# A fused linear attention and MoE kernel: the queries of batches 3 to 7 projected once, by token, and their exponentials turned by DMA transposes

## The chip, the core and the metric

The kernel runs on one core of one Trainium2 chip. The metric is the device time of one execution in microseconds (us), median of several runs. Engines are named as in the profile: PE is TensorE (PEld its weight loads), DVE is VectorE, ACT is ScalarE, POOL is GpSimd, and SP is SyncE, whose in-order queue issues nearly all DMAs.

## The reference

Attention with a feature map comes first, then a two-layer network over its output:

```
def phi(x):
    proj = np.einsum('bhsd,df->bhsf', x, w_phi)
    proj = proj - np.max(np.abs(proj), axis=-1, keepdims=True)
    return np.concatenate([np.exp(proj), np.exp(-proj)], axis=-1)
q_p, k_p = (phi(q), phi(k))
kv = np.einsum('bhsf,bhsd->bhfd', k_p, v)
z = np.sum(k_p, axis=2)
num = np.einsum('bhsf,bhfd->bhsd', q_p, kv)
den = np.einsum('bhsf,bhf->bhs', q_p, z)[..., None] + 1e-06
...
h = x @ w_in
g = h * (1.0 / (1.0 + np.exp(-1.702 * h)))
return (g @ w_out).astype(np.float32)
```

There are 8 batches, 8 heads, 576 tokens, head dimension 64 and 128 features, so phi gives 256. The second part takes 4608 tokens of 512 channels through 2048 hidden units. Here it is called the MoE, after the names of its weights.

## The kernel before

Each float32 operand is held as two f16 parts, high and low (`eh` and `el` for an exponential `e`), and a product is three f16 products: high by high, high by low, low by high.

**Attention** goes by batch and by pair of heads. `attn_load` fetches a pair's `kt`, `qt` and `vn` (512 of the 576 tokens; the last 64 tokens of all heads are done once per batch by `attn_tail`). `turned` splits `qt` or `kt` into two parts (`xs`) and turns them by one DMA transpose into `xT`, channels on partitions, eight tiles of 128 tokens. `keys` makes the sums `kz`. `queries` takes the eight tiles of queries in two halves of four. For each half, `project_q` projects **twice**. `by_token` gives the projection with tokens on partitions (eight passes of 128 columns with `xT` as weights), and VectorE takes the largest magnitude `m` of each token from it. Two further passes of 512 columns, with `ph` as weights, give the same projection turned: features on partitions, in a second PSUM bank `pT`. `features_q` takes the two exponentials of `pT` and their parts, and these serve as weights in `numden`, which multiplies them with `kz`. `token_scales` uses `m` to set each token's scale afterwards.

```
def project_q(xT, m, bank, also=()):
    pp3 = by_token(xT, bank, ())
    R.vector.tensor_reduce(m, pp3, AX.X, ALU.max, apply_absolute_value=True)
    pT = psa()
    mv = xT.rearrange("p t s -> p (t s)")
    R.tensor.matmul(pT, ph[:, 0], mv, start=True, stop=False, also=also)
    R.tensor.matmul(pT, ph[:, 1], mv, start=False, stop=True)
    return pT
```

**The MoE** goes over 384 tokens at a time (`moe_chunk`), 16 hidden blocks `j` for each: passes into a bank `hb`, then tanh (`th`) on ScalarE, `g` on VectorE, the parts `gh` and `gl`, and passes into three banks `ab`. One block `j` of one chunk is called a step here; there are 208 of them. Each step has one `g` and one `gl` instruction on VectorE, by which a place in the program can be found in any version. The attention of batches 3 to 7 is interleaved with the MoE of earlier batches.

**Order.** All instructions are first recorded (`Recorder`), then put in order by a list scheduler (`schedule`). It takes priorities from a table (`PLACES`), prices each instruction, gives out buffers, and chooses the engine where there is a choice: `two` means VectorE or GpSimd, `three` also ScalarE. Each engine then executes its instructions in that order. SP's queue too is in order: a DMA whose source isn't ready holds up all that stand behind it. `touch` finds which earlier instructions an instruction must follow.

The weights are loaded through three buffers `raw` (4 KB a partition) and two buffers `wy` (2 KB).

Of the kernel before, what the change touches and what calls it, by code (L numbers as in the profile page):

```python
# [10 lines left out]
F16 = mybir.dt.float16  # L11
# [5 lines left out]
AF = mybir.ActivationFunctionType  # L17
ALU = mybir.AluOpType
AX = mybir.AxisListType
PSUM = bass.MemoryType.PSUM  # L20

P = 128
# [3 lines left out]
LN2 = math.log(2.0)  # L26
# [4 lines left out]
class _Buf:  # L31


    def __init__(self, aps, ordered):
        self.aps, self.ordered = aps, ordered
        self.avail = [0.0] * len(aps)
        self.owner = [None] * len(aps)
        self.queue, self.head = [], 0

# [138 lines left out]
class Recorder:  # L178
# [63 lines left out]
    def claim(self, o, tl):  # L242
        if tl not in o.uses:
            if tl.first is None:
                tl.first = o
                o.allocs.append(tl)
            else:
                o.deps.setdefault(tl.first, False)
            o.uses.append(tl)
            tl.left += 1  # L250

    def touch(self, o, a, write):
        tl = a.tl
        self.claim(o, tl)
        p0, p1, rs = a.region()
        keep = []
        for ent in tl.log:
            (q0, q1, cs), w, d = ent
            hit = q0 < p1 and p0 < q1 and any(c0 < b1 and b0 < c1 for b0, b1 in rs for c0, c1 in cs)
            if hit and (w or write) and d is not o:  # L260
                o.deps[d] = True
            over = write and d is not o and p0 <= q0 and q1 <= p1
            if not (over and all(any(b0 <= c0 and c1 <= b1 for b0, b1 in rs) for c0, c1 in cs)):
                keep.append(ent)
        keep.append(((p0, p1, rs), write, o))
        tl.log = keep
# [207 lines left out]
def attn_moe_fast(ctx, tc, q, k, v, w_phi, w_in, w_out, out):  # L474
# [21 lines left out]
    U = 1.0 / PH  # L496
    EK, EQ, KZ = 3, 8, 13
# [4 lines left out]
    R = Recorder(nc)  # L502

    def buf(name, shape, dt, n, pool=cp, ordered=True):
        return _Buf(
            [pool.tile(shape, dt, tag=f"{name}{i}", name=f"{name}{i}") for i in range(n)],
            ordered,
        )

    def static(name, shape, dt):  # L510
# [12 lines left out]
        xT=([P, 8, P], F16), tl=([P, 3, NHP, D], F32), t=([P, 4, NF], F32),   # L523
        e=([P, 512], F32), eh=([P, 512], F16), el=([P, 512], F16),
# [7 lines left out]
        wy=([P, DM], F32), zt=([P, 2, NHP, 2, D], F16),  # L532
    )
    loose = ("sc", "eh", "el", "e", "n1", "cs", "rc", "mq")
    pools = {
        nm: buf(nm, sh, dt, NB[nm], ordered=nm not in loose) for nm, (sh, dt) in shapes.items()
    }

    def new(nm):
        return R.tile(pools[nm])  # L540
# [12 lines left out]
    def psa():  # L553
        return R.tile(at, whole=True)
# [98 lines left out]
    def weight_max(i):  # L653
        R.vector.tensor_reduce(
            wmx[:, i : i + 1], w16[:, i, 0], AX.X, ALU.max, apply_absolute_value=True
        )

    def w1(j, part, ct):
        return w16[:, 2 * j, part, ct * P : (ct + 1) * P]

# [29 lines left out]
    def turned(n, g=None):  # L690


        j = 8 if g is None else 4
        xs_, xT = new("xs")[:, 0:j], new("xT")[:, 0:j]
        h, l = xs_[:, :, 0], xs_[:, :, 1]
        if g is not None:
            n = halved(n, g)
            h, l = (x.rearrange("p (a j) d -> p a j d", a=2) for x in (h, l))
        R.three.copy(h, n)
        R.two.tensor_sub(l, n, h)  # L700
        R.sync.dma_start_transpose(xT, xs_.rearrange("p s i d -> p (s i d)"))
        return xT

    def by_token(xT, bank, also):
        pp = bank()
        for t in range(4):
            o = pp[:, t * NF : (t + 1) * NF]
            st = xT[:, t]
            R.tensor.matmul(o, st, ph[:, 0], start=True, stop=False, also=also)
            R.tensor.matmul(o, st, ph[:, 1], start=False, stop=True)  # L710
        return pp.rearrange("p (a f) -> p a f", a=4)
# [11 lines left out]
# [8 lines that stand above are left out]
# [33 lines left out]
    def features_q(pT, hi="eh", lo="el"):  # L764


        pr = []
        for sg in (U, -U):
            e, h, l = new("e"), new(hi), new(lo)
            R.scalar.activation(e, pT, AF.Exp, scale=sg, bias=-EQ * LN2)  # L770
            R.three.copy(h, e)
            R.two.tensor_sub(l, e, h)
            pr.append((h, l))
        return pr

    def token_scales(m, n):

        cs = new("cs")[:, :, 0:n]
        R.scalar.activation(cs[:, 0], m, AF.Exp, scale=-2.0 * U, bias=-EK * LN2)
        R.scalar.activation(cs[:, 1], m, AF.Exp, scale=-U, bias=EPD)  # L780
        return cs
# [121 lines left out]
    def numden(kz, st, mv, n, c, dst, more=()):  # L903


        nd = psa()[:, 0 : n * 2 * DV].rearrange("p (j s d) -> p j s d", j=n, s=2)
        mm = []
        for s in range(2):
            for i in range(len(st)):
                (eh, el), r = st[i][s], mv[i]  # L910
                o = nd[:, i, s] if len(st) == n else nd[:, :, s]
                a, z = (kz[:, x, r, s] for x in range(2))
                mm += [(eh, a, o), (eh, z, o), (el, a, o)]
        for w, z in more:
            mm.append((w, z, nd[:, :, 1, D + 1]))
        products(mm, (dst,))
        n1 = new("n1")[:, 0:n]
        R.evac.copy(n1, nd[:, :, 0])
        R.two.tensor_mul(n1, n1, c.unsqueeze(2).broadcast_to([P, n, DV]))
        R.vector.tensor_add(dst, nd[:, :, 1], n1)  # L920
# [57 lines left out]
    def queries(hp, qt_, kz, nt, x16, bank, g=None):  # L978


        n = 8 if g is None else 4
        w = n // 2
        nf = new("nf")[:, 0:n]
        xT = turned(qt_, g)
        m = new("mq")[:, 0:n]
        eq = [
            features_q(project_q(xT[:, h : h + 4], m[:, h : h + 4], bank, (nf,)))
            for h in range(0, n, 4)
        ]
        cs = token_scales(m, n)  # L990
        for s0, c in ((0, 3), (3, 3), (6, 2)) if g is None else ((0, 2), (2, 2)):
            sl = range(s0, s0 + c)
            numden(
                kz,
                [[[e[:, x % 4 * P : x % 4 * P + P] for e in eq[x // 4][s]] for s in range(2)]
                 for x in sl],
                [x // w for x in sl],
                c,
                cs[:, 0, s0 : s0 + c],
                nf[:, s0 : s0 + c],  # L1000
            )
        rc = new("rc")[:, 0:n]
        R.two.tensor_add(rc, nf[:, :, D], cs[:, 1])
        R.vector.reciprocal(rc, rc)
        xj = divided(nf, rc, w)
        if g is not None:
            turned_back(xj, hp, x16, g)
        else:
            xo = new("xo")
            R.three.copy(xo[:, 0], xj)  # L1010
            R.two.tensor_sub(xo[:, 1], xj, xo[:, 0])
            for t in range(2):
                R.sync.dma_start_transpose(
                    x16[:, t, hp, 0:MAIN].rearrange("p (j t) -> p j t", t=P),
                    xo[:, t].rearrange("p j c -> p (j c)"),
                )
        ratio(rc.rearrange("p (h j) -> p h j", h=2),
              nt[:, 2 * hp : 2 * hp + 2, D + 1].unsqueeze(2).broadcast_to([P, 2, w]),
              art[:, 0, 0:n].rearrange("p (h j) -> p h j", h=2))
# [170 lines left out]
    def v_att(i):  # L1190
        if i < 4:
            return VA[0][0] + VA[0][1] * i
        if i < 8:
            return VA[1][0] + (i - 4) * VA[1][1]
        return VA[2][0] + (i - 8) * VA[2][1]
# [7 lines left out]
    def attention(b):  # L1203
        u = v_att(4 * b)
        x16 = place(b)
        R.part(u - 0.01, u)
        tl = tail_load(b)
        nt = new("nt")
        R.part(u, u + 0.266)
        tail = attn_tail(b, tl, psa)  # L1210
        for hp in range(NHP):
            w = v_att(4 * b + hp)
            R.part(w, w + 0.517)
            kt, qt, vn = attn_load(b, hp)
            kf, kz = keys(b, hp, kt, vn, tail, nt, b == 1 and EXK1[hp], False, psa)
            queries(hp, qt, kz, nt, x16, psa)
            if hp == NHP - 1:
                queries_tail(nt, tail[3], x16)
# [54 lines left out]
    kept = new("x").rearrange("p t c s -> p (t c s)").bitcast(F32)  # L1273
    kept = kept[:, 0 : 4 * DM].rearrange("p (i n) -> p i n", i=4)
    attention(2)

    for part_ in range(NH):
        for c in (0, 256):
# [199 lines left out]
```

## Time and profile before

| | |
|---|---|
| time, median of 3 runs | 1052.39 us (1051.38 to 1053.2) |
| span of the profiled execution, first to last instruction | 1050.8 us |
| PE busy | 1010.8 us (96%) |
| PEld busy | 666.7 us (63%) |
| DVE busy | 734.5 us (70%) |
| ACT busy | 652.1 us (62%) |
| POOL busy | 283.4 us (27%) |
| DMA queue of SP and ACT issues, share of 16 engines | 30.8% |

The profiled execution has no timed value of its own beyond its span. The runs lie 0.6 to 2.4 us above it, the median 1.6 us. A busy share is an average over stretches with different limits, and the end of a matmul is modelled; how closely passes follow each other is read from their starts.

### The profile page before, as it was taken

The numbers are of one execution on the slowest core, as the hardware profiler recorded it, in microseconds if no ns is written. First come the engines' busy times: TensorE is split into PE (matmuls) and PEld (weight loads), VectorE is DVE, ScalarE is ACT, GpSimd is POOL, SyncE is SP. The second block draws the span as 40 slices with busy tenths as digits, with TensorE's granted clock in tenths as the row PEclk, the third lists the DMA queues.
The fourth block names the chain that finished last, engine by engine and source line by source line (L and its number), as shares of the span: only waits on it lengthen the run. The fifth ranks groups of instructions, "written<-read, shape, count | busy, mean of one in ns | idle before, by whom it ended". The sixth has DMA issues, their size and how long they took to land.

```text
span 1050.8 us, 24672 instructions
## 1 busy us (share of the span) xinstructions
PE 1010.8 (96%) x9914; PEld 666.7 (63%) x9914; DVE 734.5 (70%) x1465; ACT 652.1 (62%) x1449; POOL 283.4 (27%) x396
## 2 busy tenths in 40 slices
PE   7869799999999999999999999999999999999996
PEld 5646567778666666668664455677755665576543
DVE  5899999999999989999533226776876765232232
ACT  5989899888588878899332235565565554322321
POOL 1225656433334735454100001133211121000000
PEclk9999999999999999999999999999999999999998
DMA  9756555444235453435111012221230120000101
GB/s 236 207 184 153 130 123 148 99 120 106 51 87 101 93 137 71 117 81 123 47 31 41 1 31 51 51 77 46 51 81 21 22 51 11 14 18 1 31 1 33
DMA packets 181019, 80.92 MB, mean 77 GB/s; under 512 B 149536, under 2 KB 174240, under 8 KB 180896
## 3 DMA queue, kind: packets, MB, share of 16 engines
q1 hardware_dynamic: 177968, 78.22, 30.8%
q8 instruction: 79, 1.29, 0.5%
q10 hardware_dynamic: 2928, 1.05, 0.4%
q14 instruction: 44, 0.36, 0.1%
HBM read 45.15 MB, written 9.44 MB: 52 GB/s over the span
## 4 chain that ended last, share of the span: by engine, by line
PE 84%; ACT 7%; DVE 6%; issue 2%; DMA 1%; POOL 0%; ACTq 0%; POOLq 0%; DVEq 0%
PE ab L467 34%; PE hb L467 33%; PE at L467 16%; ACT e L467 1%; ACT x L467 1%; DVE wy L467 1%; DVE gl L467 1%; ACT eh L467 1%; DVE hb L467 1%; DVE el L467 1%; ACT w L467 1%; DMA qt<-in_q_dram 1%; ACT hb L467 0%; DVE sm L467 0%; ACT raw L467 0%
## 5 line engine op out<-in xcount | busy, mean ns | idle before, releaser
L467 PE MATMUL hb<-x,w 128*128 128x192 f16 (+3 forms) x3264 | 447.6, 279 | 1.1 <-DVE g L467 0.6
L467 PEld LDWEIGHTS <-w 128*128 128x128 f16 x3264 | 277.4, 98 | 99.6 <-issue 1.6
L467 PE MATMUL ab<-w,gh 128*128 128x512 f16 x1152 | 340.1, 379 | 0.4
L467 ACT ACTIVATE th<-hb 128x384 f32<-128x384 f32 (+1 forms) x208 | 97.0, 467 | 207.8 <-PE hb L467 206.7
L467 DVE SCALAR_TENSOR_TENSOR g<-th,hb 128x384 f32<-128x384 f32 (+1 forms) x208 | 107.7, 518 | 167.2 <-ACT th L467 165.9
L467 PE MATMUL ab<-w,gl 128*128 128x512 f16 x576 | 207.8, 379 | 1.5 <-DVE gl L467 1.4
L467 PEld LDWEIGHTS <-gh 128*128 128x128 f16 x1152 | 101.4, 97 | 95.2 <-ACT gh L467 19.9
L467 DVE SCALAR_TENSOR_TENSOR gl<-g,gh 128x384 f16<-128x384 f32 (+1 forms) x208 | 120.0, 578 | 45.8 <-ACT gh L467 45.1
L467 ACT ACTIVATE gh<-g 128x384 f16<-128x384 f32 (+1 forms) x208 | 103.8, 499 | 68.1 <-DVE g L467 65.5
L467 PEld LDWEIGHTS <-eh 128*128 128x128 f16 x1856 | 111.5, 97 | 26.8 <-ACT eh L467 3.5
L467 ACT CAST eh<-e 128x512 f16<-128x512 f32 x212 | 127.7, 623 | 1.2 <-PE at L467 0.6
L467 DVE TENSOR_TENSOR el<-e,eh 128x512 f16<-128x512 f32 x161 | 116.1, 738 | 15.3 <-ACT eh L467 10.9
L467 POOL TENSOR_TENSOR el<-e,eh 128x512 f16<-128x512 f32 x71 | 86.5, 1220 | 108.7 <-ACT eh L467 76.0
L467 PEld LDWEIGHTS <-gl 128*128 128x128 f16 x576 | 55.0, 97 | 71.4 <-DVE gl L467 31.5
L467 PE MATMUL at<-ph,xT 128*128 128x128 f16 x1024 | 94.9, 220 | 3.1 <-DVE t L467 2.2
L467 PEld LDWEIGHTS <-el 128*128 128x128 f16 x928 | 85.7, 98 | 15.0 <-DVE el L467 4.0
L467 ACT ACTIVATE e<-t 128x512 f32<-128x512 f32 x128 | 76.1, 628 | 19.9 <-DVE t L467 16.9
L467 ACT ACTIVATE e<-at 128x512 f32<-128x512 f32 x136 | 76.9, 602 | 17.7 <-PE at L467 17.1
L467 POOL TENSOR_TENSOR n<-n,cs 128x132 f32<-128x132 f32 (+1 forms) x74 | 42.5, 577 | 157.5 <-ACT n L467 142.8
L467 PEld LDWEIGHTS <-xT 128*128 128x128 f16 x1056 | 73.6, 98 | 16.4 <-issue 3.1
L467 PE MATMUL at<-kz,eh 128*128 128x66 f16 x960 | 78.7, 193 | 2.2 <-DVE x L467 1.1
L467 PE MATMUL at<-vs,eh 128*128 128x66 f16 x896 | 71.1, 194 | 0.0
(184 smaller groups left out, 1285.7 us busy)
## 6 DMA issues: line engine op xcount, KB each, us to landing
kt<-in_k_dram SPq DMA_DIRECT2D x32, 256.0 KB, 3.0
qt<-in_q_dram SPq DMA_DIRECT2D x32, 256.0 KB, 3.0
raw<-in_moe_w_in_dram SPq DMA_DIRECT2D x16, 512.0 KB, 4.2
raw<-in_moe_w_out_dram SPq DMA_DIRECT2D x16, 512.0 KB, 4.3
vn<-in_v_dram SPq DMA_DIRECT2D x62, 128.0 KB, 3.0
out_dram<-e SPq DMA_DIRECT2D x37, 128.0 KB, 2.4
out_dram<-e SPq DMA_DIRECT2D x16, 256.0 KB, 2.7
xT<-xs SPq DMA_TRANSPOSE x68, 2.8
```

Of the source, the lines that this page charges most:

```text
L467: f(*[g(a) for a in o.args], **{k: g(a) for k, a in o.kw.items()})
```

## The change

For batches 3 to 7 (32 pairs of heads less 12, so 20 pairs or 40 halves) `features_turned` takes the place of `project_q` and `features_q`. The queries are projected by token only. The exponentials are taken there, tokens on partitions, and their two parts are written side by side into one tile `hl`. One DMA transpose on SP's queue turns both parts, eight blocks of 128 by 128, into `eT`, which `numden` uses as weights. The reduction for `m` comes last, after both exponentials have read the bank. `eT` lies in the memory of `raw` (six places) and `hl` in that of `wy` (two places), so both wait for the last use of those by the weights. `touch` now also puts two reads of one PSUM tile by different engines in order. The queries of batches 0 to 2 and all tails stay as they were.

```diff
@@ claim
             if tl.first is None:
                 tl.first = o
                 o.allocs.append(tl)
+                for d in tl.buf.behind:
+                    o.deps[d] = True
@@ touch
+        bank = "PSUM" in str(a.t.space)
...
-            if hit and (w or write) and d is not o:
+            if hit and d is not o and (w or write or bank and (
+                    len(d.alts) > 1 or len(o.alts) > 1 or d.eng != o.eng)):
                 o.deps[d] = True
@@ new functions
+    def after_weights():
+
+        behind = [o for o in R.ops if any(tl.buf in (pools["raw"], pools["wy"]) for tl in o.uses)]
+        for nm, home, pat in (("eT", "raw", "p (i a t) -> i p a t"), ("hl", "wy", "p (i a t) -> i p a t")):
+            sh = dict(a=8, t=P) if nm == "eT" else dict(a=2, t=4 * P)
+            aps = [
+                ap.bitcast(F16).rearrange(pat, **sh)[i]
+                for ap in pools[home].aps
+                for i in range(ap.shape[1] * 4 // 2048)
+            ]
+            pools[nm] = _Buf(aps, True)
+            pools[nm].behind = behind
+
...
+    def features_turned(pp3, m):
+
+        pr = []
+        for sg in (U, -U):
+            e, hl, eT = new("e"), new("hl"), new("eT")
+            R.scalar.activation(
+                e, pp3.rearrange("p a f -> p (a f)"), AF.Exp, scale=sg, bias=-EQ * LN2
+            )
+            R.three.copy(hl[:, 0], e)
+            R.two.tensor_sub(hl[:, 1], e, hl[:, 0])
+            R.sync.dma_start_transpose(eT, hl.rearrange("p i n -> p (i n)"))
+            pr.append([eT[:, i : i + 4].rearrange("p a t -> p (a t)") for i in (0, 4)])
+        R.vector.tensor_reduce(m, pp3, AX.X, ALU.max, apply_absolute_value=True)
+        return pr
+
@@ queries
-        eq = [
-            features_q(project_q(xT[:, h : h + 4], m[:, h : h + 4], bank, (nf,)))
-            for h in range(0, n, 4)
-        ]
+        if "eT" in pools:
+            eq = [
+                features_turned(by_token(xT[:, h : h + 4], bank, (nf,)), m[:, h : h + 4])
+                for h in range(0, n, 4)
+            ]
+        else:
...
     attention(2)
+    after_weights()
```

Since the scheduler works anew, the order of all engines differs from batch 3 on; up to there it is the same. In all, TensorE has 80 passes of 512 columns and 80 loads of `ph` less, SP 80 transposes more, and the exponentials, copies, subtractions and reductions are as many as before.

**TensorE, last half of queries of batch 7.** In the order before, the end of the by-token projection (bank `at_65`, weights `xT`) is followed, among MoE passes (`hb`), by the two passes of 512 columns with `ph`:

```order
L467 MATMUL at_65<-ph_246,xT_83 128x128
L467 LDWEIGHTS w_248
L467 MATMUL hb_68<-x_127,w_248 128x384
L467 LDWEIGHTS ph_246
L467 MATMUL at_66<-xT_83,ph_246 128x512
L467 LDWEIGHTS w_248
L467 MATMUL hb_68<-x_127,w_248 128x384
L467 LDWEIGHTS ph_246
L467 MATMUL at_66<-xT_83,ph_246 128x512
L467 LDWEIGHTS w_248
```

In the new order of TensorE there are no such passes. The weights of `numden` are the turned parts, which lie in `raw`; this is where those of the first half of batch 7's third pair of heads come first:

```order
L472 MATMUL at_66<-ph_246,xT_83 128x128
L472 LDWEIGHTS w_248
L472 MATMUL hb_67<-x_126,w_248 128x384
L472 LDWEIGHTS raw_169
L472 MATMUL at_65<-kz_116,raw_169 128x66
L472 LDWEIGHTS gh_133
L472 MATMUL ab_69<-w_248,gh_133 128x512
```

The passes with `ph` are gone, and the turned parts are used after other passes: between the last by-token pass of that half and the row with `raw_169` stand 21 passes of 384 columns, 9 of 512 and 10 of 128. This is the shortest such distance of the 40 halves; in nine others it is 16 to 19 thousand columns, in the other 30 more.

**SP, where batch 3's queries begin.** Before, SP's queue holds loads (`tl`, `qt`, `vn`, `kt`), transposes of queries and keys (`xT<-xs`) and of finished attention (`x<-xo`) here:

```order
L467 DMA tl_84<-in_q_dram 64x4x64 x2
L467 DMA qt_76<-in_q_dram 128x2x256
L467 DMA tl_84<-in_v_dram 64x4x64 x2
L467 DMA_TRANSPOSE xT_82<-xs_80 128x8x128
L467 DMA vn_79<-in_v_dram 128x4x64 x2
L467 DMA_TRANSPOSE x_126<-xo_125 128x4x128
L467 DMA kt_73<-in_k_dram 128x2x256
L467 DMA_TRANSPOSE xT_82<-xs_81 128x8x128
```

Now the transposes of the exponentials' parts, which show as `raw<-wy`, stand among them:

```order
L472 DMA tl_84<-in_v_dram 64x4x64 x2
L472 DMA qt_76<-in_q_dram 128x2x256
L472 DMA_TRANSPOSE raw_169<-wy_172 128x8x128
L472 DMA_TRANSPOSE xT_82<-xs_80 128x8x128
L472 DMA_TRANSPOSE raw_169<-wy_173 128x8x128
L472 DMA vn_79<-in_v_dram 128x4x64 x2
L472 DMA_TRANSPOSE raw_170<-wy_172 128x8x128
L472 DMA_TRANSPOSE x_126<-xo_125 128x4x128
L472 DMA_TRANSPOSE xT_82<-xs_81 128x8x128
L472 DMA kt_73<-in_k_dram 128x2x256
```

Nothing else has left the queue; between the two transposes of a half there are other DMAs, each of which waits for its own source.

**VectorE around MoE step 86.** Before, batch 5's attention is over here, and VectorE has the MoE and small final sums alone:

```order
L467 SCALAR_TENSOR_TENSOR gl_136<-g_132,gh_134 128x384
L467 TENSOR_REDUCE vmx_240<-tl_84 128x1
L467 COPY sc_164<-vmx_240 128x8
L467 TENSOR_REDUCE sc_164<-wmx_241 128x2
L467 COPY sc_164<-phm_247 128x1
L467 SCALAR_TENSOR_TENSOR g_131<-th_129,hb_68 128x384
```

Now batch 5's attention (sums `n`, `nf`, `nt`; maxima `sm` of keys and `mq` of queries) is still going on there:

```order
L472 SCALAR_TENSOR_TENSOR gl_136<-g_132,gh_134 128x384
L472 TENSOR_TENSOR n_118<-n_118,cs_150 128x198
L472 TENSOR_TENSOR nf_120<-at_65,n_119 128x132
L472 TENSOR_TENSOR nf_120<-at_66,n_118 128x198
L472 TENSOR_TENSOR rc_163<-nf_120,cs_150 128x8
L472 TENSOR_TENSOR n_119<-n_119,cs_155 128x132
L472 RECIPROCAL rc_163<-rc_163 128x8
L472 TENSOR_TENSOR nt_122<-at_64,n_119 128x132
L472 TENSOR_TENSOR xf_123<-nf_120,rc_163 128x2x4x64
L472 TENSOR_REDUCE sm_143<-at_66 128x4
L472 TENSOR_REDUCE mq_145<-at_65 128x4
```

From step 48 to step 84 VectorE now has 361 instructions where it had 424, and from step 84 to step 96 it has 111 where it had 39.

## Rows read from the trace of the kernel before

**Rows 1.** The page, parts 1 and 2: busy us by engine, and granted clock.
```profile
PE 1010.8 (96%) x9914; PEld 666.7 (63%) x9914; DVE 734.5 (70%) x1465; ACT 652.1 (62%) x1449; POOL 283.4 (27%) x396
PEclk9999999999999999999999999999999999999998
```

**Rows 2.** Busy time by stretch: us, engines (instructions), clock, DMA share, GB/s.
```profile
0.00:200.00 200.00, 170.29 (x1665) 123.58 (x1666) 177.94 (x366) 172.04 (x390) 83.78 (x138) 0.97 0.63 160
...
281.00:505.00 224.00, 223.42 (x2769) 153.40 (x2767) 210.09 (x424) 191.81 (x434) 116.13 (x150) 1.00 0.44 101
505.00:553.00 48.00, 47.89 (x385) 32.38 (x383) 16.86 (x33) 14.73 (x30) 1.23 (x2) 1.00 0.12 30
...
640.00:870.00 230.00, 229.34 (x2344) 152.12 (x2343) 168.36 (x325) 136.88 (x303) 51.81 (x67) 1.00 0.22 51
870.00:1050.80 180.80, 171.99 (x1153) 99.52 (x1148) 57.44 (x118) 50.15 (x100) 2.17 (x4) 0.98 0.06 16
```

**Rows 3.** Waits of PE, 200 to 1050 us: us in total, times, longest.
```profile
PE at L467 <- DVE el L467: 0.5, 1, 0.5
PE ab L467 <- DVE gl L467: 0.4, 1, 0.4
PE at L467 <- ACT eh L467: 0.2, 1, 0.2
```

**Rows 4.** Timeline of PE in two stretches: start, us, operation, count.
```profile
516.99 4.12 PE L467 MATMUL hb<-x,w 128*128 128x192 f16 x48
520.95 0.81 PE L467 MATMUL ab<-w,gh 128*128 128x512 f16 x3
...
686.70 0.59 PE L467 MATMUL at<-xT,ph 128*128 128x512 f16 x2
687.13 0.49 PE L467 MATMUL hb<-x,w 128*128 128x192 f16 x4
```

**Rows 5.** Groups by form, whole run: busy us, mean ns, idle before.
```profile
L467 PE MATMUL at<-xT,ph 128*128 128x512 f16 x136 | 42.7, 384 | 0.0
L467 PEld LDWEIGHTS <-ph 128*128 128x128 f16 x136 | 12.4, 99 | 6.6 <-issue 0.3
L467 DVE TENSOR_TENSOR el<-e,eh 128x512 f16<-128x512 f32 x161 | 116.1, 738 | 15.3 <-ACT eh L467 10.9 <-PE at L467 1.9 <-POOL eh L467 1.2
L467 POOL TENSOR_TENSOR el<-e,eh 128x512 f16<-128x512 f32 x71 | 86.5, 1220 | 108.7 <-ACT eh L467 76.0 <-PE at L467 21.0 <-ACT e L467 2.8
```

**Rows 6.** Timeline of one half of queries, batch 7.
```profile
839.43 0.59 PE L467 MATMUL at<-xT,ph 128*128 128x512 f16 x2
...
840.06 1.08 ACT L467 ACTIVATE e<-at 128x512 f32<-128x512 f32 x2 [0.16 <-PE at L467]
...
841.44 0.62 ACT L467 CAST eh<-e 128x512 f16<-128x512 f32 x1
...
842.44 0.68 DVE L467 TENSOR_TENSOR el<-e,eh 128x512 f16<-128x512 f32 x1
```

**Rows 7.** Tile xT: transposes on SP, ns min/median/max, and their landing.
```profile
L467 SPq DMA_TRANSPOSE xT<-xs x68: 1194/1250/2577, 13.4 to 840.1; - x68
DMA to landing us min/median/max: 2.7/2.8/6.3
```

**Rows 8.** Timeline of SP: transposes behind each other.
```profile
421.88 1.26 SPq L467 DMA_TRANSPOSE x<-xo  x1
423.23 1.25 SPq L467 DMA_TRANSPOSE xT<-xs  x1
```

**Rows 9.** Waits of SP's queue, 281 to 870 us: us in total, times, longest.
```profile
SPq L467 <- PE at L467: 141.6, 33, 23.4
SPq L467 <- ACT e L467: 73.5, 11, 49.6
SPq L467 <- PE hb L467: 46.3, 6, 36.1
```

**Rows 10.** Tile wy: its last use.
```profile
L467 POOL TENSOR_TENSOR w<-wy,w x10: 1152/1160/1456, 88.2 to 189.9; 128x512 f16<-128x512 f32 x10
```

More of the change, by code (lines that the diff above doesn't have):

```diff
@@ L36, in __init__ @@
         self.avail = [0.0] * len(aps)
+        self.behind = ()
         self.owner = [None] * len(aps)
@@ L985, in queries @@
         m = new("mq")[:, 0:n]
-        eq = [
-            features_q(project_q(xT[:, h : h + 4], m[:, h : h + 4], bank, (nf,)))
-            for h in range(0, n, 4)
-        ]
+        if "eT" in pools:
[4 more added lines that the diff above has]
+        else:
+            eq = [
+                features_q(project_q(xT[:, h : h + 4], m[:, h : h + 4], bank, (nf,)))
+                for h in range(0, n, 4)
+            ]
         cs = token_scales(m, n)
```

## The prediction

> **What bounds the kernel now.** The page comes first: TensorE is busy 96% of the span, VectorE 70%, ScalarE 62% [rows 1]. That is an average, so the windows come next [rows 2]. Up to 200 us TensorE is idle for 30 us; there the weights are prepared and batches 0 to 2 begin, and the change touches none of it. From 281 to 505 us, where the attention of batches 3 to 5 runs beside the MoE, TensorE is busy 223.4 of 224 us and VectorE 210.1 (94%). From 640 to 870 us, where batches 6 and 7 run, TensorE has 229.3 of 230 and VectorE 168.4 (73%). The waits confirm it: from 200 us on, TensorE waits three times, 1.1 us in all [rows 3].
>
> A busy TensorE need not be one at its peak, since the ends of passes are modelled. So I read starts. In the MoE 48 passes of 192 columns start at 516.99 and the next group at 520.95 [rows 4]: 9,216 columns in 3.96 us, or 0.43 ns a column. That is 2.33 columns a nanosecond, with a granted clock of 1.00 (the 2.4 GHz level) in these stretches [rows 2]. The stream has no hidden room: what is taken out of it comes off the time, if nothing new holds it up.
>
> The Trainium skill says otherwise of the measure used first. Its page "Perfetto Trace Analysis" (Identifying the Most-Contended Engine) warns that matmul busy share is no good measure for TensorE and names the busy share of weight loads as one that is. By that share, 63% here, there would be room, and what is removed might cost nothing now: the sum would be 0 where the row on starts makes it 17 us. I go by the starts, and keep the other as a rival.
>
> **What is removed.** Each half of the queries loses two passes of 512 columns. A pair of them starts at 686.70 and the next pass at 687.13 [rows 4], so it holds TensorE for 0.43 us. (The mean of 384 ns for one [rows 5] contains a modelled end that overlaps the next pass.) There are 20 pairs of heads with two halves each: 40 × 0.43 = **17.2 us**. The 80 loads of `ph`, 99 ns each [rows 5], run on the load side beside passes of 512 columns, and I count nothing for them. The order has just these 160 instructions less on TensorE, so the change does what it says there. The passes lie between 286 and 866 us, in the saturated stretches.
>
> **What keeps its cost.** Exponentials, copies, subtractions and reductions are as many and as large as before. The scheduler gives VectorE 11 instructions more and GpSimd 11 fewer: some subtractions that took GpSimd 1.22 us take VectorE 0.74 [rows 5]. That is some 8 us for VectorE, spread over 580 us, and hidden while TensorE is the bound. A half now holds one PSUM bank through two exponentials and a reduction where it held two for less time each; I count nothing. Nor do I for the wait for the weights' buffers: their last use begins at 189.9 us [rows 10], long before the first queries of batch 3. The new order between reads of one bank mostly repeats orders that the data set already.
>
> **What is added: latency and SP's time.** A transpose of the same size is there already, `xT<-xs`. It takes SP 1.25 us to issue and lands 2.8 us after the start of its issue [rows 7]; transposes behind each other start 1.35 us apart [rows 8]. So 80 more need 100 us of SP's queue. In 281 to 870 us that queue stands waiting for 261 us on its three largest causes alone [rows 9], so there is room in total.
>
> The latency matters half by half. In one half of batch 7 the two passes start at 839.43 and the second subtraction ends at 843.12: 3.7 us [rows 6]. The projection that remains takes about as long as these passes did (1,024 columns by-token too), so from the end of it, some 3.1 us go to exponentials, copies and subtractions. With 2.8 us to land that makes **5.9 us** from the last by-token pass to weights that can be loaded; 6.4 if GpSimd does the last subtraction (0.5 us more [rows 5]).
>
> In the new order the shortest distance between these two points, in batch 7, is 21 passes of 384, 9 of 512 and 10 of 128 columns, 13,952 columns, which at 0.43 ns are 6.0 us. Nine more halves have 16 to 19 thousand columns, or 7 to 8 us, the other 30 more. So one half is just in time, nine have one or two microseconds to spare, and 30 have room. From below, this costs nothing. From above: each of the ten finds one foreign transpose ahead of its own in the queue (1.25 us) and GpSimd on the subtraction. The short one then waits 1.7 us and nine wait up to 0.7 each, 8 us together. I take 0.7 us, near the lower end, because a foreign transpose ahead has usually been issued by the time the parts are ready: SP mostly waits.
>
> The Trainium skill has a price that speaks against this. Its page "VectorE: DVE Perf Modes" (The three transpose paths) gives 1309 ns for one 128 × 128 block through the DMA transpose and 390 ns for TensorE. Eight blocks would be 10.5 us, an estimate from that page, the chain would be some 13.6 us, more than half of the halves would be late, and the time would come out on the slow side, as in the third rival. This trace has eight blocks landing in 2.8 us [rows 7], so the blocks don't queue one by one, and the row decides.
>
> **The sum.** 1050.8 − 17.2 + 0.7 = 1034.3 us for a profiled execution. The median lies 1.6 us above the span of before; so **1036 us**.
>
> **Rivals.**
> First, VectorE becomes the bound from 281 to 505 us. 24 of the 40 halves lie there, 10.3 us of TensorE's time. If VectorE's work stays in that stretch, its 210.1 us stand against 213.7: 98%, too dense for an in-order engine with dependencies, and in the worst case these halves bring nothing: 1036 + 10.3 = **1046 us**. Against it, the order moves work out of the stretch: from MoE step 48 to 84 VectorE has 361 instructions where it had 424, and the 72 more up to step 96 fall where it was busy 16.9 of 48 us [rows 2]. Over both stretches it has 227 us, some 6 more from GpSimd, of 262: 89%. It decides if VectorE's work per TensorE time rises above what the stretch shows now, 94% [rows 2].
>
> Second, no change: TensorE's stream has room that starts don't show, and the removed passes lay in it: **1052 us**. The few waits and the starts speak against it [rows 3, 4], the busy share of weight loads [rows 1] for it.
>
> Third, on the other side: transposes stand in SP's queue behind something that waits. The queue is in order, its longest wait on a store of results was 49.6 us and on TensorE 23.4 [rows 9], and the order puts stores and loads between the two transposes of a half. While the parts are late, `numden` stops TensorE, with the MoE passes queued behind it, and then VectorE and ScalarE that wait for these. If a half loses more than 17.2 / 40 = 0.43 us on average, the kernel becomes slower; at one foreign transpose each (1.25 us) without any spare it is 50 − 17.2 = 33 us over, **1085 us**. Against it: 30 of 40 halves have over 8 us for a chain of 5.9, so most must lose 2 us or more first.
>
> **Chances and range.** The forecast 0.75: TensorE stays the bound where the passes came out, and losses stay under 6 us. VectorE as bound 0.12, no change 0.04, slower 0.09. What a measurement of this kernel can tell from no change is about 0.2%, 2.1 us. The first two cases are faster by more than that: 0.87; same 0.04; slower 0.09. The forecast's own range is 1031 to 1042 us: below, 1050.8 − 17.2 without an added wait, without the 1.3 us that TensorE idles in the stretches between 281 and 870 us [rows 2], and with the smallest distance of run to span, 0.6 us, makes 1033, and I leave 2 us for losses between starts that no view sums; above stands the upper bound of waits, 1033.6 + 8, less what can't fall together. With the VectorE case the range is **1031 to 1046 us**; the two rivals left out hold 0.13.
>
> **What would show it.** In the changed profile passes `at<-xT,ph` of 512 columns must be 56 where they were 136. TensorE's busy time should fall by about 17 us, its idle time after 200 us stay near what it is, and stretches without query attention (before 281 us and after the last batch) keep their lengths. New waits of TensorE on the DMA `raw<-wy` would show the third rival, and in SP's waits what stands ahead. The first would show as TensorE waiting on VectorE's `el`, `gl` or `t` between 281 and 550 us. Wrong would be the prediction if transposes landed later than 2.8 us, or if the order left fewer columns than the parts need where SP or VectorE run behind.

## The result and the profile after

The changed kernel takes 1039.88 us (median of four runs, 1039.18 to 1041.13), the one before 1052.09 (four runs). The ratio is 0.9882, with an interval from 0.9868 to 0.9896: 12.2 us less. The forecast was 1036 us, in a range of 1031 to 1046. The mechanism came as forecast; the loss beside it is about 5 us where 0.7 was allowed.

The page after, parts 1 and 4: busy time of each engine, then the shares of the chain that ended last.

```profile
span 1037.4 us, 24731 instructions
PE 997.5 (96%) x9834; PEld 659.0 (64%) x9834; DVE 741.0 (71%) x1476; ACT 649.6 (63%) x1449; POOL 279.0 (27%) x385
...
PE 75%; DVE 12%; ACT 7%; issue 3%; DMA 2%; SPq 1%; POOL 0%; ACTq 0%; DVEq 0%; POOLq 0%
```

TensorE has 80 passes and 13.3 us of busy time less than in [rows 1]. VectorE's share of the chain is now 12%; it was 6%. Groups by form, as in [rows 5]:

```profile
L472 PE MATMUL at<-xT,ph 128*128 128x512 f16 x56 | 17.6, 396 | 0.0
```

136 of these passes have become 56. Windows after, with the columns of [rows 2]:

```profile
0.00:200.00 200.00, 172.55 (x1680) 125.12 (x1681) 177.89 (x367) 172.59 (x391) 84.40 (x141) 0.97 0.63 162
...
280.00:547.00 267.00, 262.89 (x3099) 180.77 (x3098) 234.78 (x464) 203.19 (x460) 112.39 (x145) 1.00 0.70 137
547.00:636.00 89.00, 88.87 (x495) 44.98 (x493) 29.25 (x54) 24.91 (x50) 1.51 (x3) 1.00 0.10 23
636.00:860.00 224.00, 223.26 (x2300) 148.59 (x2298) 166.46 (x326) 137.22 (x304) 52.01 (x63) 1.00 0.43 86
860.00:1037.40 177.40, 170.00 (x1151) 98.83 (x1149) 57.07 (x117) 49.77 (x99) 1.63 (x3) 0.99 0.08 20
```

Batches 6 and 7 (636 to 860 us) are as dense as before: TensorE is idle for 0.7 us. In the stretch of batches 3 to 5 (280 to 547 us) it is idle for 4.1 us, where before it was 0.7 us over 281 to 553 [rows 2]. So most of the loss lies there. The waits of TensorE, 200 to 1040 us, as in [rows 3], say on what:

```profile
PE at L472 <- DVE nf L472: 1.4, 2, 1.3
PE ab L472 <- DVE gl L472: 1.1, 2, 0.6
PE at L472 <- DVE nt L472: 1.0, 1, 1.0
PE at L472 <- DMA raw<-wy: 0.4, 1, 0.4
PE at L472 <- DVE t L472: 0.3, 1, 0.3
PE hb L472 <- DVE g L472: 0.2, 1, 0.2
```

4.0 of the 4.4 us end with a result of VectorE, which is busy for only 88% of the stretch. The new transposes (`raw<-wy`) hold TensorE up directly once, for 0.4 us; the run without them shows that the 1.0 us on `nt` begins with them too.

The largest wait and the short half of batch 7, from the timeline after:

```profile
500.67 0.68 DVE L472 TENSOR_TENSOR wy<-e,wy 128x512 f16<-128x512 f32 x1
500.69 1.67 POOL L472 TENSOR_TENSOR wy<-e,wy 128x512 f16<-128x512 f32 x1
501.26 2.48 DVE L472 TENSOR_TENSOR n<-n,cs 128x198 f32<-128x198 f32 x2
502.33 1.27 POOL L472 TENSOR_TENSOR xs<-tl,xs 128x512 f16<-128x512 f32 x1
503.67 0.55 DVE L472 TENSOR_TENSOR nf<-at,n 128x198 f32<-128x198 f32 x2
504.08 0.34 PE L472 MATMUL at<-ph,xT 128*128 128x128 f16 x3 [1.28 <-DVE nf L472]
...
823.25 0.61 PE L472 MATMUL at<-ph,xT 128*128 128x128 f16 x8
823.90 1.08 ACT L472 ACTIVATE e<-at 128x512 f32<-128x512 f32 x2
...
825.71 3.49 SPq L472 DMA_TRANSPOSE raw<-wy  x2
826.07 0.69 DVE L472 TENSOR_TENSOR wy<-e,wy 128x512 f16<-128x512 f32 x1
...
830.31 0.10 PEld L472 LDWEIGHTS <-raw 128*128 128x128 f16 x1 [0.65 <-DMA raw<-wy]
```

Above, TensorE wants to begin a by-token projection in a bank that `nf` has to read first. `nf` comes late because two additions `n<-n,cs` took 2.48 us together, where an undisturbed one takes 0.36. They end at 502.59 and 503.75, and the two GpSimd subtractions beside them at 502.36 and 503.60. Below, the short half: its first pair of parts is ready at 825.69, its second at 826.76, and TensorE loads its first weights at 830.3. These need the first transpose alone, which was issued at 825.71 and took 4.55 us to land, as the chain that ended last shows:

```profile
825.71 4.55 DMA raw<-wy
```

The second landed at 831.12, and its weights are first loaded at 832.76.

How much was lost? Idle time understates it, since a late start partly hides in the modelled length of the pass before. So I took, from the starts of all passes after 200 us, each interval to the next start, less the median of its group (same tiles and form), and summed the differences: 7.5 us before, 14.0 after. This sum is called the excess below. Where nothing differs between two kernels it hardly moves: from 200 to 280 us it is 1.12 or 1.13 us before, after, and in the three kernels that leave instructions of the change out. The same intervals give 0.216 us for a removed pass, 17.3 us for the 80. The profiled spans differ by 13.4 us, of which 1.2 come from the first 24 MoE steps, which the change doesn't touch. So some 5 us are lost by the time, and 6.5 by the excess; the 1.4 us between them is the end of the program, which from the start of the last pass took 9.15 us in the profiled execution before and 7.72 after. In the other kernels it lies between 7.6 and 9.0, so the excess is the better measure of what the order loses.

### The profile page after: what moved, and what is told of

It reads as the page before. It is cut to its first block, busy times and chain, and to the rows that moved or that the text cites. A ratio compares the mean times of both kernels' runs of the same rounds, so it can differ in the third digit from the quotient of the medians.

```text
span 1037.4 us, 24731 instructions
## 1 busy us (share of the span) xinstructions
PE 997.5 (96%) x9834; PEld 659.0 (64%) x9834; DVE 741.0 (71%) x1476; ACT 649.6 (63%) x1449; POOL 279.0 (27%) x385
## 4 chain that ended last, share of the span: by engine, by line
PE 75%; DVE 12%; ACT 7%; issue 3%; DMA 2%; SPq 1%; POOL 0%; ACTq 0%; DVEq 0%; POOLq 0%
PE ab L472 32%; PE hb L472 30%; PE at L472 13%; ACT e L472 2%; DVE gl L472 2%; DVE wy L472 1%; DVE sm L472 1%; DVE el L472 1%; DVE t L472 1%; DVE g L472 1%; DMA raw<-wy 1%; ACT x L472 1%; DVE n L472 1%; DVE hb L472 1%; DVE mq L472 1%
## 5 line engine op out<-in xcount | busy, mean ns | idle before, releaser
L472 PE MATMUL hb<-x,w 128*128 128x192 f16 (+3 forms) x3264 | 443.1, 279 | 1.4 <-DVE g L472 1.0
L472 ACT CAST eh<-e 128x512 f16<-128x512 f32 x138 | 82.6, 617 | 0.2
L472 DVE TENSOR_TENSOR el<-e,eh 128x512 f16<-128x512 f32 x110 | 78.6, 730 | 5.6 <-ACT eh L472 5.0
L472 PEld LDWEIGHTS <-eh 128*128 128x128 f16 x1216 | 70.9, 97 | 17.1 <-issue 2.3
L472 POOL TENSOR_TENSOR n<-n,cs 128x132 f32<-128x132 f32 (+1 forms) x65 | 35.5, 551 | 126.4 <-ACT n L472 122.4
L472 PE MATMUL at<-vs,eh 128*128 128x66 f16 x896 | 68.8, 194 | 0.0
L472 POOL TENSOR_TENSOR el<-e,eh 128x512 f16<-128x512 f32 x42 | 52.9, 1259 | 49.4 <-ACT eh L472 33.2
L472 PEld LDWEIGHTS <-el 128*128 128x128 f16 x608 | 56.3, 98 | 9.0 <-DVE el L472 2.4
L472 PE MATMUL at<-vs,el 128*128 128x66 f16 x448 | 55.7, 192 | 0.0
```

Source lines behind the costliest of these rows:

```text
L472: f(*[g(a) for a in o.args], **{k: g(a) for k, a in o.kw.items()})
```

## The experiments

Theory A: VectorE's own load in 281 to 550 us makes it late. Theory B: the transposes, late or crowding SP. Theory C, formed on the rows at 500 us: GpSimd's subtractions stretch VectorE's instructions, and the new order has no slack for that. "Order kept" means that the planned order of all engines stays, and only the named instructions are not issued. The runs of before beside these kernels had medians of 1050.9 to 1051.7 us.

### The transposes left out

```diff
+            if o.meth == "dma_start_transpose" and o.args[0].tl.buf is self.turns:
+                continue
...
+            a_ = [self.fixed() if isinstance(a, V) and a.tl.buf is self.turns else g(a) for a in o.args]
```

Order kept; the 80 transposes aren't issued and `numden` takes a constant tile as weights, so the queries' exponentials don't enter the output.

> The changed kernel with its order kept, but the 80 new transposes are not issued, and the products of the queries take a tile of ones as weights instead of the turned parts (so the query exponentials do not enter the output). The change gave 12.2 us where the passes removed are worth 17.2: 5 us are lost. Theory A, VectorE runs behind in the stretch of batches 3 to 5 and frees PSUM banks and MoE parts late: the loss stays, 1039 to 1040 us. Theory B, transposes come late or crowd the loads in SP's queue: without them the loss is gone, 1034 to 1036 us.

Measured: 1038.41 us, ratio 0.9877 [0.9861, 0.9892]. The waits of TensorE, 280 to 546 us:

```profile
PE at L475 <- DVE nf L475: 1.2, 2, 1.1
PE ab L475 <- DVE gl L475: 1.2, 2, 0.7
PE at L475 <- DVE t L475: 0.3, 1, 0.3
```

Without any transpose the ratio is lower by 0.0005, some 0.5 us, less than the intervals can tell from nothing. The starts tell more: the excess falls from 14.0 to 11.3 us, by 2.7. The waits on `nf`, `gl` and `t` stay; those on `raw<-wy` and the 1.0 us on `nt` are gone. What that last wait hung on stands in the timeline after:

```profile
310.67 1.26 SPq L472 DMA_TRANSPOSE raw<-wy  x1
316.09 0.62 ACT L472 CAST wy<-e 128x512 f16<-128x512 f32 x1 [1.56 <-DMA raw<-wy]
317.00 0.43 ACT L472 COPY n<-at 128x132 f32<-128x132 f32 x2
317.82 0.29 DVE L472 TENSOR_TENSOR nt<-at,n 128x132 f32<-128x132 f32 x1
318.16 0.61 PE L472 MATMUL at<-ph,xT 128*128 128x128 f16 x8 [1.05 <-DVE nt L472]
```

`hl` has two places (they show as `wy`). ScalarE can fill one again only when the transpose that reads it has landed; the one issued at 310.67 landed at 315.99. ScalarE waits 1.56 us for it, its copies of `n` and then `nt` come late, and so does TensorE. In the whole run ScalarE and GpSimd wait 12 times for a place of `hl`, 14.4 us in all; most of it costs TensorE nothing. Theory B is thus a part of the loss, though the smaller one.

### VectorE's subtractions left out

```diff
+            if o.eng == "vector" and o.meth == "tensor_sub" and o.args[0].tl.buf is self.parts:
+                continue
```

Order kept; the 48 subtractions for the low parts of the queries' exponentials that VectorE has are left out.

> The changed kernel with its order kept, but the 48 subtractions for the low parts of the query exponentials that VectorE does are left out (0.7 us each, some 30 of them in the stretch of batches 3 to 5; the low parts are then stale). Theory A, VectorE is late there: with 20 us less for it most of the loss returns, 1035 to 1037 us. Theory B, transposes are late: only these halves' chain is 0.7 us shorter, 1039 to 1040 us.

Measured: 1037.86 us, ratio 0.9873 [0.9858, 0.9888], and an excess of 12.5 us. Over 30 us of VectorE's work are gone (48 of some 0.7 us), and about 1 us comes back by the time, 1.5 by the excess. Theory A falls as the main cause.

### GpSimd's subtractions left out

```diff
+            if o.eng == "gpsimd" and o.meth == "tensor_sub" and o in self.later:
+                continue
```

Order kept; the 79 subtractions for low parts that GpSimd has from batch 3 on are left out (the tiles `hl` are zeroed once).

> The changed kernel with its order kept, but the 79 subtractions for low parts that GpSimd does from batch 3 on are left out (low parts are then stale or zero). Leaving out VectorE's own subtractions or the transposes gave back 1 us at most. Theory C: VectorE's instructions with two SBUF operands are stretched while GpSimd subtracts (n<-n,cs took 1.3 us instead of 0.37, gl 1.5 instead of 0.56), and where TensorE needs a bank or a part from them it waits. Then with these subtractions gone the 5.6 us that TensorE waits more between 281 and 550 us mostly vanish: 1033 to 1036 us. Theory D: the waits are in the order itself, whatever the engines do: 1037 to 1039 us.

Measured: 1036.03 us, ratio 0.9848 [0.9834, 0.9861], 0.34% below the changed kernel, 3.6 us; the intervals don't touch. The excess falls from 14.0 to 8.8 us. The same place in its timeline:

```profile
499.88 0.68 DVE L479 TENSOR_TENSOR wy<-e,wy 128x512 f16<-128x512 f32 x1
500.60 0.37 DVE L479 TENSOR_TENSOR n<-n,cs 128x198 f32<-128x198 f32 x1
501.24 0.30 DVE L479 TENSOR_TENSOR n<-n,cs 128x132 f32<-128x132 f32 x1 [0.28 <-ACT n L479]
501.46 0.56 DVE L479 TENSOR_TENSOR nf<-at,n 128x198 f32<-128x198 f32 x2
502.07 0.33 PE L479 MATMUL at<-ph,xT 128*128 128x128 f16 x3
```

The additions take 0.37 and 0.30 us, `nf` follows, and the projection starts without a wait. TensorE's waits, 280 to 545 us:

```profile
PE ab L479 <- ACT gh L479: 0.4, 1, 0.4
PE at L479 <- DVE mq L479: 0.3, 1, 0.3
```

The waits on `nf`, `gl`, `nt` and `t` are gone, though these are VectorE's instructions and no subtraction feeds them directly. The one on `nt` is a case of its own: without the subtractions the transposes there start earlier, and ScalarE's wait for a place of `hl` falls from 1.56 to 0.70 us. The starts of TensorE gain 1.0 us at that place, of the 5.2 in all.

### The same in the kernel before

The same two lines in the kernel before, its order kept: 80 GpSimd subtractions from batch 3 on are left out.

> The kernel before with its order kept, but the 80 subtractions for low parts that GpSimd does from batch 3 on left out (low parts stale), as a control for the same omission in the changed kernel, which gave back about 3 us. Theory C, these subtractions cost the changed order what the old order did not pay (TensorE's waits between 281 and 550 us were 1.6 us before): at most 1 us is gained, 1050 to 1051 us. Rival: they cost both kernels alike, and the 3 us say nothing of the loss: 1047 to 1048 us.

Measured: 1049.45 us, ratio 0.9987 [0.9978, 0.9996]: 1.4 us, and 1.0 us less excess (6.5). So the stretching was there before, and cost little: from 280 to 560 us alone, the excess of the kernel before falls by 0.1 us (3.0 to 2.9), that of the changed kernel by 4.6 (8.9 to 4.3). The next table counts, in 280 to 550 us, VectorE's instructions that took over 150 ns more than the median of their form, and how much more in all.

| kernel | such instructions, excess us of them | excess of TensorE, us | ratio |
|---|---|---|---|
| before | 29, 11.7 | 7.5 | 1 |
| before without GpSimd's subtractions | 8, 2.4 | 6.5 | 0.9987 |
| after | 35, 16.4 | 14.0 | 0.9882 |
| after without GpSimd's subtractions | 7, 2.0 | 8.8 | 0.9848 |
| all subtractions of the queries on GpSimd | 40, 22.8 | 18.0 | 0.9919 |

By the time of the whole kernel, GpSimd's subtractions cost the old order 1.4 us and the new one 3.6, though the stretching is of like size, 11.7 and 16.4 us. The new order lets less pass.

### All of the queries' subtractions on GpSimd

```diff
-            R.two.tensor_sub(hl[:, 1], e, hl[:, 0])
+            R.gpsimd.tensor_sub(hl[:, 1], e, hl[:, 0])
```

The order is planned anew.

> The changed kernel planned anew with all 80 subtractions of the query exponentials' low parts on GpSimd. Theory C: 48 more subtractions of 1.2 us on GpSimd stretch more of VectorE's instructions, though VectorE has 35 us less of its own work: 1040 to 1044 us. Theory A (VectorE's own load is the cause): 1035 to 1037 us.

Measured: 1043.06 us, ratio 0.9919 [0.9906, 0.9933], more stretching and more excess (table). Waits of TensorE, 280 to 552 us:

```profile
PE at L472 <- DMA raw<-wy: 2.0, 3, 1.0
PE at L472 <- DVE el L472: 1.8, 3, 0.7
PE ab L472 <- DVE gl L472: 1.2, 4, 0.4
```

The direction is theory C's, but a slower subtraction also makes each transpose later (2.0 us), so the size is not all its.

### Half of the change

```diff
-        if "eT" in pools:
+        if "eT" in pools and R.turning:
...
+        R.turning = b < 6
```

Batches 3 to 5 alone; with `b >= 6`, batches 6 and 7 alone.

> The change for batches 3 to 5 alone, 24 of 40 halves, worth 10.3 us by their passes. Theory A, the whole loss of 5 us lies here: 1047 us. Theory B, each half loses 0.13 us: 1044 to 1045 us.

> The change for batches 6 and 7 alone, 16 of 40 halves, worth 6.9 us by their passes. Theory A, the loss lies where VectorE is 94% busy, before batch 6: nearly all of it is gained, 1045 to 1046 us. Theory B, each half loses alike by its transposes (5 us over 40 halves, 0.13 us each): 1047 to 1048 us.

Measured: batches 3 to 5 alone 1047.47 us, ratio 0.9965 [0.9952, 0.9979]; batches 6 and 7 alone 1047.72, ratio 0.9963 [0.9949, 0.9976]. By passes they save 10.3 and 6.9 us; they bring 3.7 and 3.9, and 12.4 together. The sizes don't add, because each is planned anew: with batches 6 and 7 alone, the order of batches 3 to 5 changes too and waits on VectorE there (`kz` 1.5 us, `el` 0.7, `g` 0.6 in its waits). So these two runs don't locate the loss.

### The reduction ahead of the exponentials

```diff
+        R.vector.tensor_reduce(m, pp3, AX.X, ALU.max, apply_absolute_value=True)
         pr = []
...
-        R.vector.tensor_reduce(m, pp3, AX.X, ALU.max, apply_absolute_value=True)
```

> The changed kernel planned anew, with the reduction for the token maxima ahead of the exponentials instead of behind them. If the bank that is held until VectorE has reduced it is what makes TensorE wait, the time falls by some us, 1035 to 1037 us; if not, it stays within the scatter of a new order, 1037 to 1042 us.

Measured: 1040.79 us, ratio 0.9899 [0.9882, 0.9915], excess 13.9. No gain: nothing here says that the bank's being held until the last reduction makes TensorE late. As the order is planned anew, the run doesn't rule out a small part.

### Fewer subtractions on GpSimd

```diff
+    def pay(self, o, e):
+        return self.price[e] if o.soon or e != "gpsimd" else 1.4
...
-                        w += a[2] * self.price[a[0]]
+                        w += a[2] * self.pay(o, a[0])
...
```

From batch 3 on the scheduler counts GpSimd at 1.4, 1.7 or 1.9 times its cost instead of 1.247, and plans anew. GpSimd then has 62, 39 or 30 of the subtractions `el<-e,eh` and `wy<-e,wy`, where the change gives it 74. (The expectations count the tails' subtractions too; by that count the traces have 72, 48 and 35, of 84.)

> The changed kernel planned anew with GpSimd's price in the scheduler at 1.4 instead of 1.247 from batch 3 on, so that it takes 66 of the subtractions of exponentials where it took 84; all work is done. Theory C (GpSimd's subtractions stretch VectorE): 18 fewer, some 4 us less stretching against 13 us more work for VectorE: 1037 to 1039 us. Without theory C: more load on VectorE alone, 1039 to 1042 us.

> The same at a price of 1.7: 45 subtractions on GpSimd. Theory C: the stretching is about halved, 1036 to 1039 us. Without it, with 28 us more for VectorE: 1041 to 1045 us.

> The same at a price of 1.9: 35 subtractions on GpSimd. Theory C: little stretching is left, but VectorE has 35 us more work and may become the bound from 281 to 505 us: 1037 to 1042 us. Without theory C: 1043 to 1047 us.

Measured: 1044.87, 1042.09 and 1042.87 us, ratios 0.9939 [0.9925, 0.9952], 0.9911 [0.9897, 0.9924] and 0.9914 [0.99, 0.9927]. The stretching falls as meant (15.7, 10.1 and 3.1 us, from 16.4), the excess doesn't (19.3, 16.5 and 15.1). With 1.9, in 280 to 545 us, TensorE waits on other things:

```profile
PE ab L477 <- ACT e L477: 3.1, 1, 3.1
PE at L477 <- DMA raw<-wy: 1.3, 2, 0.9
PE at L477 <- DVE nt L477: 0.6, 1, 0.6
```

These miss. Theory C explains most of the loss in the order at hand; it gives no rule by which this scheduler finds a better one. Each new plan brings waits of its own, of several microseconds. What makes one plan tighter than another stays open.

### Batch 2 too

```diff
-    attention(2)
     after_weights()
+    attention(2)
```

> The change for batch 2 as well (8 more halves, 3.4 us of passes between about 200 and 260 us, where TensorE is busy 80.9 of 81 us and VectorE 76.3). If passes removed there come off the time: 1036 us; if VectorE bounds that stretch: 1039 to 1040 us.

Measured: 1044.72 us, ratio 0.9931 [0.9917, 0.9944]: some 5 us slower than the change, with 16 passes less. TensorE is busy 75.6 of the 80 us from 200 to 280 (79.9 after the change) and waits there on `raw<-wy` 1.6 us, `g` 1.4, `nf` and `kz` 0.6 each. No version with all the work in it beat the changed kernel.

## Why the prediction was right, and where it was off

**The bound and what is removed: right.** TensorE was saturated, and what went out of its stream came off the time, less the loss. 17.2 us were forecast and 17.3 measured by the starts, with nothing for the loads of `ph`. The rule of the Trainium skill ("Perfetto Trace Analysis", Identifying the Most-Contended Engine) on the busy share of weight loads, read as the prediction read it, would have given no change; that share is 64% now as it was 63%, and the kernel is 12.2 us faster. The starts were the measure to go by.

**The transposes: right in place, by luck in size.** The half that was to be just in time is the one that waits. From its last by-token pass, which ends with the exponential's start at 823.9, to its weights at 830.3 are 6.4 us; 5.9 were forecast. But the forecast let the first weights wait for both pairs of parts, and they wait for the first pair only, which was ready after 1.8 us (3.1 forecast for both). With the 2.8 us of [rows 7] the weights would have been there at 828.5, in time. They were late because this one transpose took 4.55 us to land, where the median of the 80 is 3.2; why, no run shows. It cost 0.4 us by the list of waits and 0.5 by the excess, which holds 0.6 more behind `raw<-wy` between 281 and 560 us, and some 1.2 at 318 us, where a place of `hl` came free late. With the transposes left out the excess falls by 2.7 us, so the term of 0.7 was too small; the time, 0.5 us less, can't tell the two apart. The third rival, with SP's queue blocked and the kernel slower, didn't come.

**The failed step: "the added wait is 0.7 us", with VectorE's part and the wait for the weights' buffers counted at nothing.** The excess grew by 6.5 us instead. The prediction asked only whether VectorE's total fits (89% forecast, 88% measured), and found it hidden. But TensorE waits for single results, `nf`, `gl`, `nt` and `t`, and these were late. VectorE's own work is the smaller part: 48 subtractions less brought about 1 us by the time, 1.5 by the excess. Leaving out GpSimd's subtractions, which feed none of these four directly, brought 3.6 and 5.2. In the kernel before the same brings 1.4 and 1.0. The prediction priced a move of subtractions from GpSimd to VectorE, which didn't even happen: GpSimd has 74 of `el` and `wy`, where it had 71 [rows 5], and what moved to VectorE are mostly additions (`n<-n,cs` on GpSimd from 74 to 65). What a subtraction on GpSimd does to VectorE's next instruction had no term. For the weights' buffers the prediction looked at their last use by the weights, at 189.9 us, and not at the new tiles that follow each other there: `hl` is held until its transpose has landed, which cost TensorE some 1.2 us at 318 us. Whether more places for `hl` would save that was not run. One caution: without GpSimd's subtractions the parts are also ready sooner, so the 5.2 us are not all stretching; 1.0 of them lies at 318 us and belongs to `hl`. How much else of the 5.2 comes that way was not measured.

**Of the rivals** the first named the place (281 to 550 us) and the sign (waits on `gl` and `t`), and put the price at 10.3 us; its cause, VectorE as bound, was wrong, and the price half of that. By the excess, 5.2 of the 6.5 us lost go with GpSimd's subtractions and 2.7 with the transposes; about 1 us is in both, the wait at 318 us. By the time it is 3.6 and 0.5 of 5, each known to some 2 us either way. No run leaves both out.

**What was to show it:** 56 passes, as said. Busy time of TensorE fell by 13.3 us, not 17: by 15.6 after 200 us, while in the first 200 us, which hold 15 passes more, it rose by 2.3. Modelled ends that take in part of the late starts may hide the rest. Idle time after 200 us went from 10.3 to 12.5, and up to the last MoE step from 1.5 to 5.1, so it did not stay near what it was. Stretches without the queries' attention kept their lengths; from MoE step 168 to the last the two traces agree (153.1 and 153.2 us). One sum of the range was off, without consequence: its upper end, 1033.6 + 8, is a span and leaves out the 1.6 us up to the median.

## What to carry to other kernels

Work taken out of a saturated in-order engine comes off the time, at the price of its start-to-start intervals; then ask which single results that engine will now wait for, not only whether the others' totals still fit. An instruction's duration in the row of its form is a mean or a median: look at its longest one and at what ran beside it, for a tight order pays the longest. Follow a wait back beyond the engine that it names: the one on `nt` began with a DMA that held a buffer. Check what such a buffer's next user waits for, not only its first. And in a planned kernel, changing one cost moves everything: to test a cause, keep the order and leave instructions out.

## What the runs showed of the hardware

A VectorE instruction with two operands in SBUF can be held up while GpSimd subtracts. One row of each trace, by tile (ns: least, median, longest) shows it; first after:

```profile
L472 DVE TENSOR_TENSOR n<-n,cs x59: 285/359/1321, 51.3 to 868.0; 128x198 f32<-128x198 f32 x36, 128x132 f32<-128x132 f32 x23
```

and without GpSimd's subtractions from batch 3 on:

```profile
L479 DVE TENSOR_TENSOR n<-n,cs x59: 283/358/581, 53.1 to 864.6; 128x198 f32<-128x198 f32 x36, 128x132 f32<-128x132 f32 x23
```

The median hardly changes; the longest falls from 1321 to 581 ns. `gl` reached 1528 ns where its median is 557. In the timeline at 500 us each of the two stretched additions ended 0.15 to 0.22 us after the GpSimd instruction that ran beside it, and GpSimd's own subtraction, begun behind VectorE's, took 1.67 us, where the median of its form is 1.16. From 280 us on, 50 VectorE instructions of the changed kernel took over 150 ns more than the median of their form. A GpSimd instruction ran beside every one, in 38 cases a subtraction. Of the 50, 49 read two tiles in SBUF and one was a copy; of the 190 VectorE instructions that read PSUM beside a GpSimd instruction, none was stretched. The Trainium skill says this in "SBUF — State Buffer" (Who interferes with whom): a VectorE instruction with two inputs in SBUF contends with a GpSimd instruction that reads SBUF, and whichever comes second is blocked until the other ends. The rows agree, in both directions.

Transposes of the same size landed in different times. The page's median from issue to landing, after:

```profile
raw<-wy SPq DMA_TRANSPOSE x80, 3.2
```

`xT<-xs` has 2.8 us in [rows 7], and 3.0 in the changed kernel. Single ones of `raw<-wy` took up to 5.3 us. Why is open.
